# Spreading a feature DFT over the main loop of a DFT-and-attention kernel, one group a round, with sixteen pairs of sequence DFT a round behind it

## The chip, the core and the metric

The kernel runs on one core of a Trainium2 chip. The metric is the device time of one execution in microseconds. The kernel before the change took 1862.16 us, the median of 3 runs (1861.99 to 1862.94). The work is done by five engines with a queue each: PE (matrix products), DVE (vector work), ACT (activations), POOL (general elementwise work) and SP, which issues all transfers here. Each engine takes its queue strictly in order.

## The reference

```
# x: S=2048 tokens, D=640 features; 32 heads of width 20, one shared k and v
a = einsum("bsd,ed->bse", x, dft_hid_re)          # feature DFT
b = einsum("bsd,ed->bse", x, dft_hid_im)
A = einsum("ts,bse->bte", dft_seq_re, a) - einsum("ts,bse->bte", dft_seq_im, b)
q, k, v = x @ wq, x @ wk, x @ wv                  # q in 32 heads
p = softmax(q k^T / sqrt(20))
B = (p v, heads joined) @ wo
g = sigmoid((x * gate_w).sum(-1))
return g * A + (1 - g) * B
```

## The kernel before, in words

Precision comes from splitting each factor into a high and a low part in a 32-bit format that PE multiplies fast; a product is three matmuls (high by high, high by low, low by high). Half-height matmuls with 64 rows of weights run in pairs, one in the upper and one in the lower row group of PE; in the code, `y0` and `y1` are the two halves of one such pair. The order on PE, ACT, DVE and POOL is the order of the program; that of the transfers on SP (all issued by `move`, L106) is chosen by the framework's scheduler.

The stages are these. First come the projections q, k, v and the gate (L114 to L116). Then comes the feature DFT (`ab`, L125): 16 token tiles, 4 groups each of 15 pairs of 64x320 matmuls; between them run the first score maxima. The main loop has 256 rounds: 16 pairs of heads, two halves of the queries (qh) and 8 steps over the keys (kk). A round holds:

- `b` (`b_unit`, L647): eight score products of 512 columns; ACT takes the exponential (L655) into `pt`.
- `a` (`a_unit`, L319): eight score products for the next pair of heads, of which DVE takes the row maxima (L326). The exponentials need those maxima first, since they are subtracted inside `b` as two more rows of `qs`.
- `y` (L551): 12 pairs of the sequence DFT, 64x320 each, with coefficients `ch` and `cl` that POOL splits (L397, L398) from `craw`. A y block is 128 tokens of output with four series of eight tiles; 96 pairs, in two passes (`sh`) over halves of the input tokens. `E` copies out a finished block (ACT L556), and POOL adds (L561, in the second pass also L565).
- `V` (`av_step`, L659): the products of `pt` with v, full height, two per round, which stand apart.

`ROUND` (L737) is the list of these steps, written by hand; `ROUND_LAST` serves the last pair of heads, which has no `a`, and splits each V in half-height steps `W` (L676). Scores go to five banks named S0 to S4, `y` to F0 and F1, V to one bank.

The maxima of a pair of heads are ready when its last `a` is reduced. `a_reduce` and then `a_final` (L336) run some ticks later, a tick being a fixed step of the round: a transpose on DVE (`mt`), a cast and a subtraction on POOL (`ms`, L341 and L342), a write to DRAM (`m_d`) and four reads back into rows 60, 61, 124 and 125 of `qs` (L349). `LEAD` = 12 says by how many units of `a` the maxima run ahead of the loop; four units are a round. `load_c` loads and splits a coefficient tile. It uses three slots in turn, and is called after the first and after the third series of a block for the next block. The slot of the second call is that of a tile which the block's fourth series still reads.

After the loop the output stage multiplies by wo (L114 to L116).

Of the kernel before, what the change touches and what calls it, by code (L numbers as in the profile page):

```python
# [33 lines left out]
def kernel(  # L34
# [46 lines left out]
    m_d = dram.tile([NPAIR, P, 2, 32], F32, name="m_d")  # L81
# [48 lines left out]

    cw = ExitStack()
    w2 = cw.enter_context(tc.tile_pool(name="w2", bufs=1, side="right"))
    x2 = cw.enter_context(tc.tile_pool(name="x2", bufs=2, side="right"))
    wh, wl = [], []

    def load_w(i):
        w_v = (wrT, wiT)[i].rearrange("(c p) n -> p c n", p=P)
        h = w2.tile([P, KC, D], F32R, name=f"wh{i}")
        l = w2.tile([P, KC, D], F32R, name=f"wl{i}")
        for c in range(KC):  # L140
            raw = w2.tile([P, D], F32, name="wraw", bufs=2)
            move(raw, w_v[:, c])
            split(raw, h[:, c], l[:, c])
        wh.append(h)
        wl.append(l)


    T2 = list(range(SJ, NT)) + list(range(SJ))
    xraw, xspl = {}, {}

    def load_x2(it):
        if it < NT:
            t = T2[it]
            xraw[it] = x2.tile([P, KC, P], F32, name="xr2")
            move(xraw[it], xT_v[:, :, t * P : (t + 1) * P])

    def split_x2(it):
        if it < NT:
            h = x2.tile([P, KC, P], F32R, name="xh2")
            l = x2.tile([P, KC, P], F32R, name="xl2")  # L160
            split(xraw.pop(it), h, l)
            xspl[it] = (h, l)


    with ExitStack() as c1:
# [78 lines left out]
        for c in range(KC):  # L244
            if c:
                load_x1(0, c)
            raw = w2.tile([P, D], F32, name="wraw", bufs=2)
# [15 lines left out]
        for n in range(1, 4):  # L263
# [7 lines left out]
            if n == 3:  # L271
                load_x2(0)
                load_x2(1)
                split_x2(0)
# [6 lines left out]
            if n < 3:  # L281
                load_w(n - 1)
# [10 lines left out]
    qsp = ctx.enter_context(tc.tile_pool(name="qsp", bufs=1))  # L293
    sml = ctx.enter_context(tc.tile_pool(name="sml", bufs=2))

    qs = {}
    qbuf = [qsp.tile([P, S], F32R, name=f"qs{i}") for i in range(3)]

    def load_qs(p):
        t = qbuf[p % 3]  # L300
        qs[p] = t
        for hh in range(2):
            r = slice((2 * p + hh) * DH, (2 * p + hh + 1) * DH)
            b = 64 * hh
            move(t[b : b + 20], qh_d[r])
            move(t[b + 20 : b + 40], qh_d[r])
            move(t[b + 40 : b + 60], ql_d[r])

    mx = {}

    def a_unit(u, hh, tag="A"):

        p, r = divmod(u, 64)
        qb, c = divmod(r, 4)
        if r == 0 and p not in mx:
            mx[p] = sml.tile([P, 2, NT, 4], F32, name="mx")
# [4 lines left out]
            qs[p][b : b + 60, qb * P : (qb + 1) * P],  # L321
# [4 lines left out]
        nc.vector.tensor_reduce(mx[p][:, hh, qb, c : c + 1], ps, axis=AX.X, op=ALU.max)  # L326

    mxr = {}

    def a_reduce(p):  # L330
        mxr[p] = sml.tile([P, 2 * NT], F32, name="mxr")
        nc.vector.tensor_reduce(
            mxr[p], mx.pop(p).rearrange("p h q c -> p (h q) c"), axis=AX.X, op=ALU.max
        )

    def a_final(p):  # L336
# [3 lines left out]
        nc.vector.transpose(mt, mxr.pop(p))  # L340
        nc.gpsimd.tensor_copy(ms[:, 0], mt)  # L341
        nc.gpsimd.tensor_tensor(ms[:, 1], mt, ms[:, 0].bitcast(F32), op=ALU.subtract)  # L342
        move(m_d[p], ms)

        m_v = m_d[p].rearrange("(g h b) i t -> h i b g t", g=4, h=2)
        for hh in range(2):
            for i in range(2):
                r = 64 * hh + 60 + i
                move(qs[p][r : r + 1].rearrange("o (b g t) -> o b g t", g=4, t=32), m_v[hh, i : i + 1])  # L349
# [18 lines left out]
    def a_half(hh, tag="A"):  # L368
# [7 lines left out]
        if u % 64 == 16 and u // 64 + 1 < NPAIR:  # L376
            load_qs(u // 64 + 1)
# [12 lines left out]
    def load_c(sh, tb, i):  # L390
# [8 lines left out]
        return h, l  # L399

    first_c = {}


    ab = {}
    later_ab = []
# [472 lines left out]
```

## Time and profile before

| | us |
|---|---|
| median of 3 runs | 1862.16 |
| span of the profiled execution | 1860.4 |
| PE busy | 1846.3 |
| DVE busy | 1449.3 |
| ACT busy | 1269.3 |
| POOL busy | 391.9 |
| reduces of the maxima (L326, 2048) | 1316.3 |

The profiled execution shows one run, 1.8 us under the median. PE's row counts the time in which any matmul runs; two half-height matmuls that overlap count once. A row of the time line gives start, length, engine, line of the source, operation, output from inputs, shapes and, in brackets, the idle time ahead of it with what ended it. In the table by stage a row is a window, its length, the busy time (with counts) of PE, its weight loads, DVE, ACT and POOL, the granted clock, and the transfers' share and rate.

### The profile page before, as it was taken

The page shows a single profiled execution, that of the slowest core. Times are in us where ns is not written, and L with a number is a line of the kernel's source. Part 1 is how long each engine was busy: PE and PEld are TensorE (multiplying, and loading weights), DVE is VectorE, ACT ScalarE, POOL GpSimd, SP SyncE. Part 2 cuts the span into 40 slices and gives each one's busy share as a digit, 9 for nine tenths or more (in the row PEclk, how much of TensorE's full clock was granted, in tenths as well). Part 3 has the DMA queues.
Part 4 walks back from the last instruction along what each step waited for, and adds up shares of the span by engine and source line. Part 5 has one row for each costly group of instructions (what it writes and reads, how often), then busy time and mean ns, then how long its engine had stood idle before and what let it go on. Part 6 is the DMA issues. An engine that isn't in the chain of part 4 may idle for free.

```text
span 1860.4 us, 42326 instructions
## 1 busy us (share of the span) xinstructions
PE 1846.3 (99%) x17368; PEld 1228.9 (66%) x17368; DVE 1449.3 (78%) x2307; ACT 1269.3 (68%) x2425; POOL 391.9 (21%) x336
## 2 busy tenths in 40 slices
PE   8999999999999999999999999999999999999999
PEld 6799986566566656656655665665566566566689
DVE  4469988888888888888888888888888888883144
ACT  4333357777777777777777777777777777778830
POOL 0033431111111111111111222222222212221132
PEclk9999999999999999999999999999999999999999
DMA  7684111211112021212114412121212121111366
GB/s 246 180 262 169 42 37 41 58 42 49 51 33 67 26 61 30 57 33 63 37 56 156 172 50 64 49 65 49 64 49 61 46 65 49 44 49 39 94 203 231
DMA packets 89023, 150.64 MB, mean 81 GB/s; under 512 B 21620, under 2 KB 58484, under 8 KB 86308
## 3 DMA queue, kind: packets, MB, share of 16 engines
q1 hardware_dynamic: 88828, 147.93, 25.8%
q8 instruction: 136, 2.23, 0.5%
q14 instruction: 59, 0.48, 0.1%
HBM read 103.91 MB, written 48.23 MB: 82 GB/s over the span
## 4 chain that ended last, share of the span: by engine, by line
PE 96%; DMA 2%; SPq 1%; DVE 1%; ACT 0%; issue 0%; POOL 0%; ACTq 0%; DVEq 0%
PE av L659 26%; PE y L551 23%; PE b L647 16%; PE a L319 16%; PE ab L125 7%; PE av L676 2%; PE o L114 1%; PE o L116 1%; PE o L115 1%; SPq L106 1%; PE q L116 1%; PE q L114 1%; PE q L115 0%; DMA ql_d<-ql 0%; DMA wraw<-in_wiT_dram 0%; DMA wraw<-in_wrT_dram 0%
## 5 line engine op out<-in xcount | busy, mean ns | idle before, releaser
L326 DVE TENSOR_REDUCE mx<-a 128x1 f32<-128x512 f32 x2048 | 1316.3, 686 | 217.1 <-PE a L319 124.3
L655 ACT ACTIVATE pt<-b 128x512 f32<-128x512 f32 x2048 | 1099.7, 599 | 358.6 <-PE b L647 352.5
L319 PE MATMUL a<-ks,qs 60*128 60x512 f32 x2048 | 755.8, 430 | 0.2 <-ACT pt L655 0.2
L551 PE MATMUL y<-ab,ch 64*128 64x320 f32 x4096 | 688.2, 307 | 1.2 <-DVE both L441 1.2
L647 PE MATMUL b<-qs,ks 62*128 62x512 f32 x2048 | 685.2, 407 | 0.7 <-ACT pt L655 0.7
L551 PEld LDWEIGHTS y<-ab,ch 64*128 64x128 f32 x4096 | 569.5, 186 | 12.8 <-DVE both L441 1.5
L659 PE MATMUL av<-pt,vsb 128*32 128x512 f32 x3840 | 511.3, 605 | 0.0
L647 PEld LDWEIGHTS b<-qs,ks 62*128 62x128 f32 x2048 | 331.8, 187 | 219.0 <-ACT pt L655 218.2
L319 PEld LDWEIGHTS a<-ks,qs 60*128 60x128 f32 x2048 | 335.0, 184 | 198.9 <-ACT pt L655 198.2
L551 PE MATMUL y<-ab,cl 64*128 64x320 f32 x2048 | 456.0, 308 | 0.0
L551 PEld LDWEIGHTS y<-ab,cl 64*128 64x128 f32 x2048 | 347.1, 187 | 0.8
L659 PEld LDWEIGHTS av<-pt,vsb 128*32 128x32 f32 x3840 | 76.0, 108 | 154.8 <-issue 146.5
L561 POOL TENSOR_TENSOR yt<-yt,yu 128x320 f32<-128x320 f32 x64 | 56.8, 888 | 575.6 <-ACT yt L556 563.2
L397 POOL CAST ch<-craw 128x1024 fp32r<-128x1024 f32 x62 | 64.4, 1039 | 477.1 <-PE a L319 441.3
L398 POOL TENSOR_TENSOR cl<-craw,ch 128x1024 fp32r<-128x1024 f32 x62 | 147.7, 2383 | 5.0
L125 PE MATMUL ab<-wh,xh 64*128 64x320 f32 x640 | 134.6, 308 | 1.5 <-DVE gz L235 1.1
L125 PE MATMUL ab<-wl,xh 64*128 64x320 f32 x640 | 134.1, 306 | 0.0
L125 PE MATMUL ab<-wh,xl 64*128 64x320 f32 x640 | 133.8, 306 | 0.0
L410 POOL TENSOR_TENSOR ab<-both,ab 128x320 fp32r<-128x320 f32 x64 | 60.3, 948 | 189.5 <-DMA craw<-in_cre_dram 99.9
L125 PEld LDWEIGHTS ab<-wh,xl 64*128 64x128 f32 x640 | 96.4, 185 | 0.0
L125 PEld LDWEIGHTS ab<-wl,xh 64*128 64x128 f32 x640 | 96.2, 185 | 0.0
L440 ACT ACTIVATE half<-ab 128x320 f32<-128x320 f32 x64 | 28.0, 437 | 88.4 <-PE ab L125 88.4
(86 smaller groups left out, 967.3 us busy)
## 6 DMA issues: line engine op xcount, KB each, us to landing
craw<-in_cre_dram SPq DMA_DIRECT2D x32, 512.0 KB
craw<-in_cim_dram SPq DMA_DIRECT2D x32, 512.0 KB
qs<-qh_d SPq DMA_DIRECT2D x64, 160.0 KB
ab_d<-ab SPq DMA_DIRECT2D x16, 640.0 KB
y_d<-yt SPq DMA_DIRECT2D x64, 160.0 KB
ab<-ab_d SPq DMA_DIRECT2D x16, 640.0 KB
xr<-in_xT_dram SPq DMA_DIRECT2D x20, 256.0 KB
xr<-in_xT_dram SPq DMA_DIRECT2D x16, 320.0 KB
```

Of the source, the lines that this page charges most:

```text
L114: nc.tensor.matmul(ps, wh, xh, start=(i == 0), stop=False)
L125: nc.tensor.matmul(ps, w[r], x[r], start=(i == 0 and k == 0), stop=(i == n - 1 and k == 2))
L319: nc.tensor.matmul(ps, qs[p][b : b + 60, qb * P : (qb + 1) * P], ks[b : b + 60, c * ROW : (c + 1) * ROW], start=True, stop=True,)
L326: nc.vector.tensor_reduce(mx[p][:, hh, qb, c : c + 1], ps, axis=AX.X, op=ALU.max)
L397: eng.tensor_copy(h, raw)
L398: eng.tensor_tensor(l, raw, h.bitcast(F32), op=ALU.subtract)
L410: nc.gpsimd.tensor_tensor(lo, both, hi.bitcast(F32), op=ALU.subtract)
L551: nc.tensor.matmul(ps, w, x, start=start, stop=stop)
L561: nc.gpsimd.tensor_tensor(yt, yt, yu, op=ALU.add)
L647: nc.tensor.matmul(ps, ks[b : b + 62, kc * P : (kc + 1) * P], qs[p][b : b + 62, qc * ROW : (qc + 1) * ROW], start=True, stop=True,)
L655: nc.scalar.activation(t, ps, AF.Exp, scale=SCALE)
L659: nc.tensor.matmul(ps[32 * g : 32 * g + 32, :], vsb[:, kc, :], t, start=first, stop=last)
```

## The change

The feature DFT is now a stream of 64 groups of 15 pairs, ordered in four phases by half of the tokens and half of the columns (`ab_stream`). Sixteen groups run ahead of the loop with 80 `a`; the other 48 run in the first 48 rounds, one in each. After them come 144 rounds with 16 pairs of `y` (three rounds for half a block, six for a block), then 12 pairs a round: 54 rounds with `a`, 10 without. There are four lists: AB15, Y16, Y12 and N12. In each the two V stand side by side at the end. The last pair of heads uses V too, and W is gone. Weights and tokens of the feature DFT are loaded and split per phase, the splits on POOL. Sums of a group (`ab_sum`) are made on POOL after two ACT copies.

The maxima now run by half pairs, v = 2 x pair + query half, 32 of them, 8 rounds each. `qs` has four buffers of half the length. `LEAD` is 8 units, `a_reduce` comes one tick and `a_final` two ticks after the last `a`, and a tick is now every second `b`.

The core of the diff:

```diff
-    m_d = dram.tile([NPAIR, P, 2, 32], F32, name="m_d")
+    m_d = dram.tile([2 * NPAIR, P, 2, 32], F32, name="m_d")
...
-        if u % 64 == 16 and u // 64 + 1 < NPAIR:
-            load_qs(u // 64 + 1)
-        if u % 64 == 63:
-            later(1, a_reduce, u // 64)
-            later(3, a_final, u // 64)
+        v, r = divmod(u, UV)
+        if r == 8 and v + 1 < 2 * NPAIR:
+            load_qs(v + 1)
+        if r == UV - 1:
+            later(1, a_reduce, v)
+            later(2, a_final, v)
...
+    def ab_sum(grp):
+        t0, t1 = grp["t"]
+        half, e, t, i, hi, lo = grp["ab"]
+        nc.gpsimd.tensor_tensor(t0, t0, t1, op=ALU.add)
+        if stage["loop"]:
+            nc.gpsimd.tensor_copy(hi, t0)
+        else:
+            nc.scalar.activation(hi, t0, AF.Copy)
+        nc.gpsimd.tensor_tensor(lo, t0, hi.bitcast(F32), op=ALU.subtract)
...
+    Y16 = (
+        "b0S1 a1S0 a0S3 b1S4 y0 y1 y0 y1 y0 y1 y0 y1 y0 b1S2 y0 a1S1 y0 y0 a1S0 y0 b1S4 y0 y0 y1 y0 b1S3 y0 y1 "
+        "a0S2 y1 b0S1 y1 y1 y0 y1 y0 y1 b0S4 y1 a0S0 y1 y1 b0S3 y1 a0S2 y1 a1S1 y0 E0 E1 V V"
+    ).split()
...
+    LEAD = 8
+    NL = 2 * (UV + LEAD)
+    KL = 15 * 2 * SJ
...
+    NAB = 3 * 2 * SJ
+    Y3 = 48
+
+    def plan_of(n):
+        if n < NAB:
+            return AB15
+        if n < NAB + 3 * Y3:
+            return Y16
+        return Y12 if state[1] < NA else N12
```

`load_c` keeps its three slots and its two calls per block.

Three places in the order of instructions follow. On PE before, at the end of a round, with `av` the V products (now L734), `a` (now L368) and `b` (now L722) the scores:

```order
L319 MATMUL a_0_7568<-ks,qs_865 128x512 [waits Activation_49]
L659 MATMUL av_0_7110<-pt,vsb 32x512 x4
L319 MATMUL a_0_7575<-ks,qs_865 128x512 [waits Activation_49]
L319 MATMUL a_1_7583<-ks,qs_865 128x512 [waits DVE_49]
L647 MATMUL b_13_1_0_7586<-qs_867,ks 128x512 [waits Activation_49]
L647 MATMUL b_13_0_1_7590<-qs_867,ks 128x512
L659 MATMUL av_0_7110<-pt,vsb 32x512 x4
L647 MATMUL b_13_1_1_7598<-qs_867,ks 128x512 [waits Activation_49]
```

And in the changed kernel, at the end of round 71, with the last y's of a block ahead of the V's and the first b of half pair v = 9 behind them:

```order
L541 MATMUL y_3_1_1_9371<-ab_5044,ch 128x320
L368 MATMUL a_0_9653<-ks,qs_108 128x512 [waits DVE_49]
L541 MATMUL y_3_1_1_9371<-ab_5044,cl 128x320
L368 MATMUL a_1_9657<-ks,qs_108 128x512 [waits Activation_49]
L541 MATMUL y_3_1_0_9370<-ab_5044,cl 128x320
L734 MATMUL av_0_9045<-pt,vsb 32x512 x8
L722 MATMUL b_0_2_0_9675<-qs_107,ks 128x512 [waits DMAHW1_49,DMAHW0_49,DVE_49]
L368 MATMUL a_1_9679<-ks,qs_108 128x512
L368 MATMUL a_0_9682<-ks,qs_108 128x512 [waits Activation_49]
L722 MATMUL b_0_2_1_9691<-qs_107,ks 128x512 [waits DMAHW3_49,DMAHW2_49]
```

The two av stand together; the b behind them waits for two transfers, the reads of the maxima.

On POOL before, around the maxima of a pair, `ch` and `cl` being the split of a coefficient tile and `yt` the sum of a block's halves:

```order
L397 CAST ch<-craw 128x1024 [waits DMAHW5_49]
L398 TENSOR_TENSOR cl<-craw,ch 128x1024 [waits Pool_49]
L561 TENSOR_TENSOR yt<-yt,yu 128x320 [waits DMAHW6_49,Activation_49]
L341 CAST ms<-mt 128x32 [waits DVE_49]
L342 TENSOR_TENSOR ms<-mt,ms 128x32 [waits Pool_49]
L397 CAST ch<-craw 128x1024 [waits DMAHW3_49,PE_49]
L398 TENSOR_TENSOR cl<-craw,ch 128x1024 [waits PE_49,Pool_49]
```

On POOL now, around the maxima of half pair 9 (round 70):

```order
L551 TENSOR_TENSOR yt<-yt,yu 128x320 [waits DMAHW2_49,Activation_49]
L442 CAST ch<-craw 128x1024 [waits DMAHW2_49,PE_49]
L443 TENSOR_TENSOR cl<-craw,ch 128x1024 [waits PE_49,Pool_49]
L387 CAST ms<-mt 128x32 [waits DMAHW1_49,DVE_49]
L388 TENSOR_TENSOR ms<-mt,ms 128x32 [waits Pool_49]
L551 TENSOR_TENSOR yt<-yt,yu 128x320 [waits DMAHW3_49,Activation_49]
```

The two ms rows have moved from ahead of the ch that waits for PE to behind it and its cl.

On SP before, the four reads of the maxima (1x64x32) stand right behind their write:

```order
L106 DMA m_d<-ms 128x64 [waits DMAHW5_49,Pool_49]
L106 DMA qs_865<-m_d 1x64x32 [waits DMAHW6_49,DMAHW5_49]
L106 DMA qs_865<-m_d 1x64x32 [waits DMAHW7_49]
L106 DMA qs_865<-m_d 1x64x32 [waits DMAHW0_49]
L106 DMA qs_865<-m_d 1x64x32 [waits DMAHW1_49]
```

On SP now, for half pair 25 in the second pass over the tokens, where `y_d<-yt` writes a block's sum and `y_23491` loads the first pass's part of another:

```order
L106 DMA m_d<-ms 128x64 [waits DMAHW0_49,Pool_49]
L106 DMA y_d<-yt 128x320 [waits DMAHW1_49,Pool_49]
L106 DMA y_23491<-y_d 128x320 [waits DMAHW2_49]
L106 DMA craw<-in_cim_dram 128x1024
L106 DMA qs_107<-m_d 1x32x32 [waits DMAHW4_49,DMAHW0_49]
L106 DMA qs_107<-m_d 1x32x32 [waits DMAHW5_49]
L106 DMA qs_107<-m_d 1x32x32 [waits DMAHW6_49]
L106 DMA qs_107<-m_d 1x32x32 [waits DMAHW7_49]
```

Three transfers stand between the write and the reads now; in the first pass it is two, the sum's write (to `y0_d`) and a craw.

More of the change, by code (lines that the diff above doesn't have):

```diff
@@ L148 @@
[L148 to L162, printed above, removed]
+    qsp = ctx.enter_context(tc.tile_pool(name="qsp", bufs=1))
@@ L568 @@
     ended = []
+    stage = {"loop": False}
+    def ab_sum(grp):
[4 more added lines that the diff above has]
+            nc.gpsimd.tensor_copy(hi, t0)
+        else:
+            nc.scalar.activation(hi, t0, AF.Copy)
+        nc.gpsimd.tensor_tensor(lo, t0, hi.bitcast(F32), op=ALU.subtract)
+        if half == 1 and i == 1:
+            j = t - SJ
+            later(3, move, ab_d[j, e], ab[j, e].rearrange("p a b -> p (a b)"))
     def y_evict(g):
@@ L594, in f_stream @@
     def f_stream():
+        yield from ab_stream()
+        cw.close()
+        yp.append(ctx.enter_context(tc.tile_pool(name="yp", bufs=2, side="right")))
         cur = {}
```

390 lines of the change are left out of this document (217 added, 173 removed).

## The prediction

> **What bounds the kernel now.** I read the page's busy shares first.
>
> ```profile
> PE 1846.3 (99%) x17368; PEld 1228.9 (66%) x17368; DVE 1449.3 (78%) x2307; ACT 1269.3 (68%) x2425; POOL 391.9 (21%) x336
> ```
>
> Then the busy time by stage (window; its length; busy time of PE, weight loads, DVE, ACT and POOL; clock; DMA).
>
> ```profile
> 0.00:98.60 98.60, 90.92 (x406) 71.97 (x406) 41.00 (x65) 38.88 (x71) 4.06 (x10) 1.00 0.73 219
> 98.60:257.40 158.80, 157.26 (x2043) 156.73 (x2043) 135.25 (x237) 61.87 (x144) 62.75 (x67) 1.00 0.40 128
> 257.40:1704.20 1446.80, 1445.93 (x13408) 878.76 (x13408) 1224.81 (x1942) 1098.23 (x2071) 289.40 (x241) 1.00 0.19 57
> 1704.20:1783.50 79.30, 79.28 (x1001) 50.53 (x1001) 15.47 (x18) 68.54 (x138) 14.77 (x12) 1.00 0.37 114
> 1783.50:1860.40 76.90, 72.89 (x513) 70.90 (x512) 32.77 (x46) 1.77 (x4) 20.94 (x9) 1.00 0.67 219
> ```
>
> PE waits nowhere in the loop: 1445.93 us busy of 1446.80. The stages are projections, feature DFT with the first maxima, 240 rounds, the last pair's 16 rounds, and output: 98.6 + 158.8 + 1446.8 + 79.3 + 76.9 = 1860.4, the profiled execution. The median of the runs, 1862.16, lies 1.8 above; I add that at the end. While PE is the bound, a round costs what its matmuls cost in order, so I read one round.
>
> ```profile
> 284.31 1.07 PE L659 MATMUL av<-pt,vsb 128*32 128x512 f32 x8
> 285.30 0.50 PE L319 MATMUL a<-ks,qs 60*128 60x512 f32 x2
> 285.64 0.41 PE L647 MATMUL b<-qs,ks 62*128 62x512 f32 x2
> 285.97 1.07 PE L659 MATMUL av<-pt,vsb 128*32 128x512 f32 x8
> 286.97 0.50 PE L647 MATMUL b<-qs,ks 62*128 62x512 f32 x1
> ...
> 290.34 0.64 PE L659 MATMUL av<-pt,vsb 128*32 128x512 f32 x4
> ```
>
> The price of a half-height pair comes from the DFT stage, the first and last of forty rows:
>
> ```profile
> 99.18 0.31 PE L125 MATMUL ab<-wh,xh 64*128 64x320 f32 x2
> ...
> 104.90 0.31 PE L125 MATMUL ab<-wh,xh 64*128 64x320 f32 x2
> ```
>
> And once, where the last pair begins, two V's already stand together:
>
> ```profile
> 1706.32 1.92 PE L659 MATMUL av<-pt,vsb 128*32 128x512 f32 x16
> 1708.17 0.50 PE L647 MATMUL b<-qs,ks 62*128 62x512 f32 x2
> ```
>
> Half-height matmuls run in two row groups at once. Forty rows of L125 from 99.18 to 104.90 give 5.72 / 39 = 0.1467 us for a pair 320 wide; 512 wide is 1.6 times that, 0.2347. A V takes 0.99 (284.31 to 285.30) or 1.00. Between the V's stand two a and two b, 0.469 by that price, but 0.67 pass: 0.20 is lost where half-height work drains into a V. The other piece, 286.97 to 290.34, is 12 y pairs and 6 of 512: 1.760 + 1.408 = 3.17, again 0.20 short of 3.37. Round: 290.34 - 284.31 = 6.03. Two V's side by side occurred once: 1708.17 - 1706.32 = 1.85.
>
> **The sum without new waits.** The two V's together spare one drain and 0.14 more: a round costs (pairs x 0.1467) + (a's and b's per row group x 0.2347) + 0.20 + 1.85. Bounds of the gain are 0.14 (no drain spared) and 0.34. I take 0.34, since both pieces show the drain.
>
> - 48 rounds of 15 feature pairs, 8 per row group: 2.20 + 1.88 + 2.05 = 6.13, together 294.2.
> - 144 rounds of 16 pairs: 6.275, together 903.6.
> - 54 rounds of 12: 5.69, together 307.3.
> - 10 rounds of 12 without a's: 4.75, together 47.5.
>
> That is 1552.6 for all 256 rounds. Ahead of them remain 240 pairs and 80 maxima. PE would need 240 x 0.1467 + 40 x 0.2347 = 44.6, but DVE reduces longer:
>
> ```profile
> 631.46 2.10 ACT L655 ACTIVATE pt<-b 128x512 f32<-128x512 f32 x4 [0.36 <-PE b L647]
> ...
> 631.50 1.95 DVE L326 TENSOR_REDUCE mx<-a 128x1 f32<-128x512 f32 x3 [0.42 <-PE b L647]
> ```
>
> The loop's start, on PE:
>
> ```profile
> 257.41 0.42 PE L551 MATMUL y<-ab,ch 64*128 64x320 f32 x2 [1.19 <-DVE both L441]
> ```
>
> Three in a row take 1.95, 0.65 each, so 80 take 52. In the loop, 8 reduces are 5.2 and 8 exponentials (2.10 for four) 4.2; both fit under 5.69, DVE with little to spare. At the loop's start the kernel waits 1.19 now. Afterwards the sums and splits of feature groups go through POOL, and ACT's copy waits there ahead of the exponentials. Four casts and subtractions of the next weights stand ahead of one sum; from POOL's rows below (1.04 and 2.38 at 1024 wide) I scale them to about 5.4, so 5.5, with bounds 1 and 8. The splits during the rounds hide under PE: POOL is busy 289 of 1446.8. Projections and output stay, 98.6 and 76.9: the two left-over V's equal the four W halves.
>
> Sum: 98.6 + 52 + 5.5 + 1552.6 + 76.9 = 1785.6, 74.8 below the execution. The last W's go at no cost, since the round formula holds V's instead.
>
> **The new wait.** A half pair's maxima leave DVE (mt), pass POOL (ms), go to DRAM (m_d) and come back as rows of qs, which the first b reads. The order shows the cast ch and subtraction cl ahead of ms on POOL whenever the second coefficient load of a y block falls into the round of a_final. That ch overwrites a slot which the block's last y still reads.
>
> ```profile
> 591.86 1.04 POOL L397 CAST ch<-craw 128x1024 fp32r<-128x1024 f32 x1 [21.47 <-PE a L319]
> 592.98 2.38 POOL L398 TENSOR_TENSOR cl<-craw,ch 128x1024 fp32r<-128x1024 f32 x1
> 595.31 0.88 POOL L561 TENSOR_TENSOR yt<-yt,yu 128x320 f32<-128x320 f32 x1
> ```
>
> PE's V right behind, and then the maxima's chain on POOL and SP elsewhere:
>
> ```profile
> 592.06 0.64 PE L659 MATMUL av<-pt,vsb 128*32 128x512 f32 x4
> ...
> 629.08 0.21 POOL L341 CAST ms<-mt 128x32 fp32r<-128x32 f32 x1 [10.40 <-DVE mt L340]
> 629.37 0.25 POOL L342 TENSOR_TENSOR ms<-mt,ms 128x32 fp32r<-128x32 f32 x1
> 629.65 0.34 SPq L106 DMA_DIRECT2D m_d<-ms  x1
> 631.15 2.51 SPq L106 DMA_DIRECT2D qs<-m_d  x4
> ```
>
> The landing of another small read, and what single issues cost SP:
>
> ```profile
> 1753.01 1.17 SPq L106 DMA_DIRECT2D sm<-sum_d  x2
> 1755.92 0.25 DVE L727 RECIPROCAL rc<-sm 128x16 f32<-128x16 f32 x1 [12.94 <-DMA sm<-sum_d]
> 1138.10 0.90 SPq L106 DMA_DIRECT2D craw<-in_cre_dram  x2
> 1176.89 0.42 SPq L106 DMA_DIRECT2D y<-y_d  x1
> ```
>
> ch waited 21.47 us for PE (the named a is only the last event before it; the block's last y's go out just ahead of V). Before, ms stood in front of that ch, with a whole pair's period aligned to two blocks, so the wait hurt nobody. Now the maxima are ready two rounds before b, but ms lies behind ch until the block ends, and where that round is the fifth of six (16-pair rounds) or the seventh of eight (12-pair rounds), the block ends exactly where b must start. Half pair v has a_final in round 8v - 2. Blocks of six start at round 48: v = 9, 12, 15, 18, 21, 24 coincide. Blocks of eight start at 192: all of v = 25 to 30. That is 12 stalls; the last one splits on DVE and is free.
>
> One stall, from T, where ch starts (591.86, 0.2 before V at 592.06): b's natural place is T + 0.16 + 1.85 = 2.0. ch and cl end near 3.5, ms at 4.0. SP issues m_d; the first read follows 631.15 - 629.65 = 1.5 later. Before it stand, on SP, y0_d behind yt (0.88) and a craw (0.45): reads start at 5.8. Two reads are 2 x 0.63, their landing 1.2 (m_d's own: 1.50 - 0.34), so b starts at 8.25, and the other row group's b makes 0.65 more: 6.9 late. In the second y half the sum has one more POOL step (0.88) and y0's load (0.42): 7.7. Three of 6.9, one of 7.5 and one of 8.2 (the reload of ab and a longer queue), seven of 7.7: 90.3. Bounds: 5.5 each (one read, no queue ahead) and 9.5 (landing as for sm: 1755.92 - 1753.01 - 1.17 = 1.74 on both trips, one more sum), 66 and 114.
>
> Behind the late b stand a's and y's on PE, ACT's exponentials and DVE's reduces; nothing else feeds PE, so each stall is an idle PE. What a matmul costs after such an idle, the start shows:
>
> ```profile
> 5.85 0.79 PE L114 MATMUL kv<-xh,kvgh 128*128 128x512 f32 x1 [5.85 <-ACT kvgh L109]
> ...
> 9.43 0.58 PE L116 MATMUL q<-xh,wql 128*128 128x512 f32 x1
> 9.84 0.39 PE L114 MATMUL q<-xh,wqh 128*128 128x512 f32 x1
> 10.07 0.40 PE L115 MATMUL q<-xl,wqh 128*128 128x512 f32 x1
> ```
>
> After 5.85 us of idle, nine matmuls take 9.84 - 5.85 = 3.99, 0.44 each; then one takes 0.23. That lost 3.99 - 9 x 0.233 = 1.9 us. Whether the idle or the program's start made it, the trace can't tell: bounds 0 and 1.9 per stall. My idles are 6.2 us and more, so I take 1.9: 12 x 1.9 = 22.8. The granted clock reads 1.00 in the first window all the same, so that row doesn't show this slowness.
>
> The Trainium skill, in "TensorE: Matmul & The Clock Gate", section "Part 1: The HAM clock gate", says that an idle window of about 3.4 us halves PE's clock, and about 3.4 us of activity restores it. By that each stall would lose an estimated 1.7, 20 in all in place of 22.8; it agrees with the row at the start and speaks for the upper bound.
>
> Sum: 1785.6 + 90.3 + 22.8 = 1898.7, and 1.8 for the median: **1900**. Bounds of the unknown terms around it: stalls -24 / +24, slow restart -23, loop start -4 / +3.
>
> **The rivals.**
> - *No slow restart.* The start's slowness belongs to the start alone: 1785.6 + 90.3 + 1.8 = 1878. For it: nothing later in the trace shows slow matmuls, though no idle there comes near 6 us. Chance 0.17.
> - *The chain is short, the gain stays.* The place is SP's queue between ms and b. The stalls decide: the gain of 74.8 is gone at 6.2 us each, all told. At the lower bound of 5.5 and no slow restart the time is 1785.6 + 66 + 1.8 = 1853, faster; if the reads overlap other work still more, down to 1787 with none. For it: the two trips have been measured only apart. Against: ch and cl alone take 3.5. Chance 0.15, 0.11 of it faster, 0.04 within 0.2%.
> - *Rounds get longer.* DVE has 5.2 of 5.69 us, five banks serve 16 scores between two pairs of V. A wait of 0.12 per round gives 31 more: 1931. Against: PE idles 0.87 in the whole present loop (1446.80 - 1445.93), with banks as few. Chance 0.12.
> - *The change doesn't do what it says.* The V pair spares no drain (0.14 per round): 0.20 x 246 = 49 more, 1949. Against: the row at 1706.32. Chance 0.05.
>
> **How the numbers follow.** The forecast, 1875 to 1925 by its bounds, has 0.51. Something like 0.2% (3.7 us) is what a measurement of this kernel can tell from no change; slower sums to 0.51 + 0.17 + 0.12 + 0.05 = 0.85, same 0.04, faster 0.11. The range 1857 to 1932 leaves out the short chain and the lost drain, some 0.18.
>
> **What would show it.** PE's waits for qs rows at b about 12 times, 6 to 8 us each, every third half pair at first and each of the last six; on POOL ms starting right after a cl that waited for PE; rounds between stalls of 6.13, 6.28, 5.69 and 4.75; the loop's first b near 98.6 + 52. After a stall matmul pairs near 0.28 in place of 0.147 for some 4 us, or not. I am wrong if b doesn't wait (then near 1787), if stalls last under 5 us, or if PE waits in ordinary rounds.

## The result and the profile after

The changed kernel took 1943.76 us, the median of 4 runs (1941.94 to 1945.78), beside 1862.45 for the kernel before on the same chip: a ratio of 1.0438 (95% interval 1.0423 to 1.0452). The forecast was 1900, in a range of 1857 to 1932, and the result lies above it: the sign was right, the size about half. The profiled execution spans 1944.0, 45.3 more than the 1898.7 that the steps added up to.

The page of the changed kernel, with each engine's busy time and the granted clock in 40 slices:

```profile
PE 1817.1 (93%) x17112; PEld 1318.4 (68%) x17112; DVE 1377.8 (71%) x2249; ACT 1236.5 (64%) x2420; POOL 568.3 (29%) x561
...
PEclk9998999999999999999899899999989999888999
```

PE is busy for 29 us less than before, with 256 matmuls fewer, and yet the span is 84 us longer: PE now waits. The dips in the clock mark where. The stages, in the columns of the table before (projections; feature DFT with the first maxima; its 48 rounds; the 144 rounds with 16 pairs; 12 pairs; the last pair of heads; output):

```profile
0.00:102.70 102.70, 92.72 (x388) 72.51 (x390) 40.66 (x53) 32.47 (x60) 22.04 (x24) 0.97 0.67 212
102.70:159.18 56.48, 47.57 (x553) 45.78 (x550) 49.70 (x88) 23.94 (x55) 38.39 (x41) 1.00 0.44 145
159.18:466.60 307.42, 303.05 (x3012) 216.68 (x3016) 245.90 (x405) 242.81 (x494) 187.19 (x223) 0.98 0.24 75
466.60:1431.70 965.10, 919.04 (x9212) 656.87 (x9208) 731.25 (x1198) 648.58 (x1266) 228.75 (x199) 0.97 0.21 68
1431.70:1792.50 360.80, 308.17 (x2746) 209.61 (x2746) 243.92 (x409) 226.32 (x424) 59.84 (x58) 0.92 0.13 41
1792.50:1872.00 79.50, 78.02 (x753) 48.69 (x751) 36.77 (x58) 61.74 (x123) 16.09 (x13) 1.00 0.37 118
1872.00:1944.00 72.00, 68.55 (x469) 68.21 (x465) 29.60 (x44) 0.60 (x1) 16.04 (x6) 1.00 0.64 206
```

Some 46 us of PE's idle time lie in the fourth stage and 53 in the fifth, where before it idled 0.87 in the whole loop. The last row starts at the end of the left-over V pair; from the first product of the output, at 1867.83, it takes 76.2, near the 76.9 forecast. What PE waits for, from the list of waits (engine and line, releaser, total, count, longest):

```profile
PE b L722 <- DMA qs<-m_d: 101.2, 15, 10.5
```

Twelve of these 15 waits are the stalls that the prediction counted, v = 9, 12, 15, 18, 21, 24 and 25 to 30, of 6.55 to 10.49 us, 98.3 together; two of the others belong to the loop's start, and one of 0.39 lies in round 176. The first, from the time line (SPq rows are SP's own queue; a group's length is that of its issues):

```profile
610.46 1.04 POOL L442 CAST ch<-craw 128x1024 fp32r<-128x1024 f32 x1 [16.40 <-PE y L541]
611.58 2.35 POOL L443 TENSOR_TENSOR cl<-craw,ch 128x1024 fp32r<-128x1024 f32 x1
613.88 0.21 POOL L387 CAST ms<-mt 128x32 fp32r<-128x32 f32 x1
614.16 0.25 POOL L388 TENSOR_TENSOR ms<-mt,ms 128x32 fp32r<-128x32 f32 x1
614.44 0.35 SPq L106 DMA_DIRECT2D m_d<-ms  x1
615.25 0.34 SPq L106 DMA_DIRECT2D y_d<-yt  x1
615.64 0.42 SPq L106 DMA_DIRECT2D craw<-in_cre_dram  x1
616.17 2.77 SPq L106 DMA_DIRECT2D qs<-m_d  x4
619.14 0.76 PE L722 MATMUL b<-qs,ks 62*128 62x512 f32 x1 [6.55 <-DMA qs<-m_d]
```

ch waited 16.40 us for the block's last y; ms follows right behind cl; the write, two other transfers and the four reads follow on SP; then b goes out. And the clock around this stall (window, length, the five busy times, clock, transfers):

```profile
612.00:614.00 2.00, 0.59 (x8) 0.00 (x0) 0.05 (x1) 0.00 (x0) 2.00 (x2) 1.00 0.05 20
616.00:618.00 2.00, 0.00 (x0) 0.00 (x0) 0.00 (x0) 0.00 (x0) 1.92 (x2) 0.94 0.86 293
618.00:620.00 2.00, 0.86 (x3) 0.50 (x3) 0.02 (x1) 0.00 (x0) 0.63 (x1) 0.50 0.19 59
620.00:622.00 2.00, 1.99 (x13) 1.69 (x14) 1.26 (x2) 1.19 (x2) 0.00 (x0) 0.50 0.90 305
622.00:624.00 2.00, 2.00 (x16) 2.00 (x15) 0.94 (x2) 0.69 (x2) 0.00 (x0) 0.50 0.13 47
624.00:626.00 2.00, 2.00 (x23) 2.00 (x22) 1.30 (x3) 1.84 (x4) 0.00 (x0) 0.85 0.00 0
```

PE idles from 612.6, the clock halves a little before 618 and comes back after 624. At 0.50 PE starts 13 and 16 matmuls in 2 us, against 23 later. All told, a round with a stall lasts 9.47 to 12.54 longer than an ordinary one; the twelve sum to 124.6, that is 98.3 of idle and 26.3 behind it.

Ordinary rounds, measured from V pair to V pair, take 6.15 (15 pairs; forecast 6.13), 6.27 (16; 6.275), 4.745 (12 without a's; 4.75), but 6.05 with 12 pairs and a's, where 5.69 was forecast. One such round, on PE, DVE and ACT:

```profile
1437.74 1.92 PE L734 MATMUL av<-pt,vsb 128*32 128x512 f32 x16
...
1440.16 4.89 DVE L375 TENSOR_REDUCE mx<-a 128x1 f32<-128x512 f32 x8 [1.18 <-PE a L368]
1440.19 4.33 ACT L730 ACTIVATE pt<-b 128x512 f32<-128x512 f32 x8 [1.74 <-PE a L368]
...
1443.79 0.64 PE L734 MATMUL av<-pt,vsb 128*32 128x512 f32 x4
```

PE shows no wait here: its loss is spread in small pieces. DVE makes its eight reduces without a gap, starts 0.57 after the V pair's end (1437.74 + 1.85) and has idled 1.18 ahead of them; 4.89 and some 1.17 are the 6.05. ACT does likewise, 4.33 and 1.74.

Last, the stretch ahead of the loop: a wait in the projections, DVE's first reduces, two waits at the loop's first b's, and the exponentials behind ACT's copy of a group, which waits for POOL's sum.

```profile
57.36 0.50 PE L114 MATMUL kv<-xh,kvgh 128*128 128x512 f32 x1 [2.15 <-ACT xh L109]
...
106.66 15.04 DVE L375 TENSOR_REDUCE mx<-a 128x1 f32<-128x512 f32 x25 [2.38 <-DMA qs<-qh_d]
...
159.18 0.47 PE L722 MATMUL b<-qs,ks 62*128 62x512 f32 x1 [1.69 <-DMA qs<-m_d]
160.57 0.76 PE L722 MATMUL b<-qs,ks 62*128 62x512 f32 x1 [0.88 <-DMA qs<-m_d]
...
163.95 0.47 ACT L569 ACTIVATE ab<-abt 128x320 fp32r<-128x320 f32 x1 [5.75 <-POOL abt L565]
...
164.96 0.79 PE L368 MATMUL a<-ks,qs 60*128 60x512 f32 x1 [2.16 <-ACT pt L730]
```

The first feature group starts at 101.71; the steps let the projections end at 98.6, which makes 3.1. From there to the loop's first b, at 159.18, it takes 57.5 where the steps have 52, 5.5 more: the 80 reduces take 52, but the first starts only at 106.66. The first V pair of the loop starts at 176.12. The steps give 98.6 + 52 + 5.5, and 8.6 for the first round, which has no V pair yet, and the second up to its own; so it comes 11.4 late.

So the 45.3 us are 54 x 0.36 = 19.4 for the 12-pair rounds, 124.6 - 113.1 = 11.5 for the stalls, 11.4 ahead of the loop, and 3 in small pieces. In these 3 a slip of the sum is taken off: it has a V pair in each of the 256 rounds and one more in the output, 257 where the kernel has 256, so 1.85 too much.

### The profile page after: what moved, and what is told of

Read it like the earlier page. It is cut to its first block, busy times and chain, and to the rows that moved or that the text cites. A ratio compares the mean times of both kernels' runs of the same rounds, so it can differ in the third digit from the quotient of the medians.

```text
span 1944.0 us, 42803 instructions
## 1 busy us (share of the span) xinstructions
PE 1817.1 (93%) x17112; PEld 1318.4 (68%) x17112; DVE 1377.8 (71%) x2249; ACT 1236.5 (64%) x2420; POOL 568.3 (29%) x561
## 4 chain that ended last, share of the span: by engine, by line
PE 88%; POOL 4%; DMA 4%; SPq 2%; issue 1%; DVE 1%; ACT 0%; POOLq 0%; DVEq 0%
PE av L734 23%; PE y L541 21%; PE b L722 18%; PE a L368 14%; PE ab L541 7%; DMA qs<-m_d 2%; SPq L106 2%; POOL cl L443 2%; PE o L114 1%; PE o L115 1%; PE o L116 1%; PE q L114 1%; PE q L116 1%; PE q L115 1%; DMA wraw<-in_wq_dram 1%
## 5 line engine op out<-in xcount | busy, mean ns | idle before, releaser
L722 PE MATMUL b<-qs,ks 62*128 62x512 f32 x2048 | 790.4, 423 | 104.1 <-DMA qs<-m_d 101.2
L368 PE MATMUL a<-ks,qs 60*128 60x512 f32 x2048 | 742.0, 419 | 5.2 <-DVE mx L375 3.0
L541 PE MATMUL y<-ab,ch 64*128 64x320 f32 x4096 | 735.9, 312 | 0.0
L722 PEld LDWEIGHTS b<-qs,ks 62*128 62x128 f32 x2048 | 361.3, 190 | 331.1 <-DVE mx L375 173.6
L541 PE MATMUL y<-ab,cl 64*128 64x320 f32 x2048 | 519.7, 311 | 0.0
L734 PE MATMUL av<-pt,vsb 128*32 128x512 f32 x4096 | 492.5, 598 | 0.0
L368 PEld LDWEIGHTS a<-ks,qs 60*128 60x128 f32 x2048 | 360.8, 189 | 12.3 <-ACT pt L730 3.3
L734 PEld LDWEIGHTS av<-pt,vsb 128*32 128x32 f32 x4096 | 106.8, 109 | 223.6 <-issue 215.1
L565 POOL TENSOR_TENSOR abt<-abt,abu 128x320 f32<-128x320 f32 x64 | 55.8, 872 | 185.3 <-ACT abu L587 185.3
L541 PE MATMUL ab<-wbh,xh 64*128 64x320 f32 x256 | 60.4, 309 | 0.0
L541 PE MATMUL ab<-wbh,xl 64*128 64x320 f32 x256 | 60.1, 308 | 0.0
L570 POOL TENSOR_TENSOR ab<-abt,ab 128x320 fp32r<-128x320 f32 x64 | 56.1, 877 | 13.1 <-ACT ab L569 7.0
L541 PE MATMUL ab<-w0h,xl 64*128 64x320 f32 x192 | 49.6, 316 | 4.2 <-POOL xl L218 4.2
L541 PE MATMUL ab<-w0l,xh 64*128 64x320 f32 x192 | 51.4, 311 | 0.0
L541 PE MATMUL ab<-w1l,xh 64*128 64x320 f32 x192 | 50.9, 306 | 0.0
```

The costliest lines, as they stand in the source:

```text
L368: nc.tensor.matmul(ps, qs[v][b : b + 60, qb * P : (qb + 1) * P], ks[b : b + 60, c * ROW : (c + 1) * ROW], start=True, stop=True,)
L541: nc.tensor.matmul(ps, w, x, start=start, stop=stop)
L565: nc.gpsimd.tensor_tensor(t0, t0, t1, op=ALU.add)
L570: nc.gpsimd.tensor_tensor(lo, t0, hi.bitcast(F32), op=ALU.subtract)
L722: nc.tensor.matmul(ps, ks[b : b + 62, kc * P : (kc + 1) * P], qs[2 * p + qc // 2][b : b + 62, (qc % 2) * ROW : (qc % 2 + 1) * ROW], start= ...
L734: nc.tensor.matmul(ps[32 * g : 32 * g + 32, :], vsb[:, kc, :], t, start=first, stop=last)
```

## The experiments

**The stalls: maxima split on DVE.** The theory says that they come from ms standing behind ch on POOL, so ms goes to DVE.

```diff
-        nc.gpsimd.tensor_copy(ms[:, 0], mt)
-        nc.gpsimd.tensor_tensor(ms[:, 1], mt, ms[:, 0].bitcast(F32), op=ALU.subtract)
+        nc.vector.tensor_copy(ms[:, 0], mt)
+        nc.vector.tensor_tensor(ms[:, 1], mt, ms[:, 0].bitcast(F32), op=ALU.subtract)
```

> The changed kernel with one edit: the cast and the subtraction that make ms of a half pair's maxima run on DVE, right behind the transpose, so they no longer stand behind the ch and cl that wait for PE. Theory (ms behind ch on POOL is what delays the first b of 12 half pairs; each costs 8.2 us of idle and about 2.2 of slow clock behind it, 124.6 us in all by the length of the 12 rounds): the 12 waits vanish, 1944 - 125 = 1819 us, with the clock at 1.00 in the loop. Rival (the chain of DRAM write and reads on SP, not POOL, is too long for two rounds of lead): the waits stay at 6 us or more, over 1930 us.

1843.79 us, ratio 0.9900 (0.9886 to 0.9915) to the kernel before; the twelve long waits are gone. Of the 25 us missing to the expectation most are given back in the rounds of `a_final`. One of them, in DVE's rows and PE's V pairs:

```profile
1419.83 1.92 PE L734 MATMUL av<-pt,vsb 128*32 128x512 f32 x16
...
1423.46 0.20 DVE L386 STREAM_TRANSPOSE mt<-mxr 128x32 f32<-128x32 f32 x1
1423.69 0.18 DVE L387 CAST ms<-mt 128x32 fp32r<-128x32 f32 x1
1423.91 0.19 DVE L388 TENSOR_TENSOR ms<-mt,ms 128x32 fp32r<-128x32 f32 x1
...
1426.42 1.07 PE L734 MATMUL av<-pt,vsb 128*32 128x512 f32 x8
```

That round takes 6.59 in place of 6.05; over the half pairs it is 0.45 to 1.35 each, some 19 together. Two rounds whose first b still waits 0.6 to 0.7 for the reads (v = 19 and 22) give 2.3 more, and the loop's first V pair starts at 177.95, 1.8 later than in the changed kernel. Half a microsecond of DVE between reduces lengthens the round by as much: a first sign that DVE has no slack there.

**The stalls: a longer lead.** `ms` stays on POOL and behind ch, but a round earlier.

```diff
-    LEAD = 8
+    LEAD = 12
```

> The changed kernel with one number changed: maxima run ahead by 12 units (three rounds) in place of 8 (two). Theory (a third round of slack takes the chain off the path, and in the 12-pair part the maxima then come ahead of the second coefficient load): no waits of b over 1 us in the loop; 16 more reduces ahead of the loop cost 16 x 0.65 = 10, two rounds of 6.05 turn into two of 4.75, so 1944 - 125 + 10 - 3 = 1826 us. Rival (the order on POOL doesn't matter, the chain as such is too long by a fixed time): waits fall by one round of 6 us only, to 2 or 3 us each, about 1860 us.

1823.47, ratio 0.9793 (0.9778 to 0.9807), and no b waits for qs in the rounds. Taking away the stalls, and with them the idle and the slow restart, is worth 120 us, near the 124.6 to which the longer rounds sum up; the loop's first V pair comes 1.8 later, behind the 16 maxima more.

**The slow restart.** Matmuls without use fill the gaps, so that PE is busy through each stall.

```diff
+    FILL = {8 * v: 26 if v < 18 else 32 for v in (9, 12, 15, 18, 21, 24, 25, 26, 27, 28, 29, 30)}
...
+        fill = FILL.get(ROUNDS.index(rnd) + 1, 0)
+        if fill:
+            spin = psum.tile([P, ROW], F32, tag="F0", name="spin", bufs=1)
+            for i in range(fill):
+                nc.tensor.matmul(spin, ks[:, :P], ks[:, :ROW], start=True, stop=True)
```

> The changed kernel with 26 or 32 extra matmuls of 128x512 (0.23 us each at full clock, 6.1 or 7.5 us) into an idle bank at the end of each of the 12 rounds ahead of a late b; their result is read by nothing. Theory (after an idle of 6 us and more the clock falls to half and stays there for over 5 us, which costs 2.2 us a time; the extra matmuls fit into the idle and keep the clock up): granted clock 1.00 behind these rounds, 12 x 2.2 = 26 less, 1918 us. Rival (the slow restart is the refill of DVE and ACT and not the clock): no gain, 1944 us or above.

1931.03, 12.7 less than the changed kernel; the ratio to before is 1.0368 (1.0348 to 1.0389). Two of the windows of above, in this kernel:

```profile
618.00:620.00 2.00, 1.03 (x5) 0.32 (x4) 0.39 (x1) 0.38 (x1) 0.30 (x1) 1.00 0.27 61
620.00:622.00 2.00, 1.99 (x23) 2.00 (x25) 1.31 (x3) 1.42 (x3) 0.00 (x0) 1.00 0.82 301
```

The clock stays at 1.00, and 23 matmuls start where 13 did. From the late b to the next V pair, summed over the twelve, 76.9 has become 57.6: 19.4 of the 26.3 were the clock, although in two stalls 2.1 and 3.3 us stayed unfilled and the clock still fell. The waits themselves grew by 2.8, so the total fell by less than expected. That the idle makes the slow restart is shown.

**The V pair by itself.** The kernel before with the list Y12 of the changed one, so only the rounds' order is new.

```diff
-        "y0 y1 y0 a1S0 b0S2 y1 b1S3 y0 y0 y1 y0 y1 y0 a1S1 y0 b0S4 y1 y1 y0 y1 y0 y1 y0 y1 "
-        "a0S2 y1 y1 b0S3 a1S0 y0 y0 y1 b1S1 E1 a0S4 V a0S3 a1S0 E0 b0S1 b1S2 V b1S1 a0S4"
+        "b0S0 a1S3 a0S4 y1 y1 b0S1 y1 y0 b1S2 y1 y0 y0 a1S0 b0S3 y1 y0 y1 y0 a1S1 y0 y0 b1S4 y0 y1 y0 a1S2 "
+        "b0S0 y0 y1 y1 a0S3 y1 b1S4 a0S1 y0 y1 y1 y0 b1S2 a0S0 E0 E1 V V"
```

> The kernel before with one edit: its round's list is the 12-pair list of the change, with the two V side by side; everything else stays (feature DFT ahead of the loop, whole pairs of maxima, lead of 12). Theory (with the V's together no score can be made for 1.85 us, so 16 scores have to pass five banks in the rest of the round; DVE and ACT set that, and a round of 12 pairs can't fall under 6.05 us): no gain, 240 x (6.05 - 6.03) = +5, 1867 us. Rival (the prediction's formula, a round costs its matmuls and one drain): 240 x 0.34 less, 1781 us.

1872.51, ratio 1.0056 (1.0039 to 1.0073).

```profile
503.95 1.92 PE L659 MATMUL av<-pt,vsb 128*32 128x512 f32 x16
...
510.03 1.92 PE L659 MATMUL av<-pt,vsb 128*32 128x512 f32 x16
```

6.08 from pair to pair, where V's apart gave 6.03. At 12 pairs the gain of 0.34 doesn't appear. (The list also places y and the banks differently, so this alone doesn't say that the V pair is the reason.) The next runs ask why. Each changes `lead_12`, so that no stall interferes, and all but `v_apart` only in its 12-pair rounds.

**Is it DVE?** Reduces over 256 of 512 columns.

```diff
-        nc.vector.tensor_reduce(mx[v][:, hh, qb, c : c + 1], ps, axis=AX.X, op=ALU.max)
+        wide = HALF_ROW[0]
+        nc.vector.tensor_reduce(mx[v][:, hh, qb, c : c + 1], ps[:, :wide], axis=AX.X, op=ALU.max)
```

> The kernel of lead_12 with one edit: in the rounds of the 12-pair list with a's, DVE reduces only the first 256 of the 512 columns of each score tile (the maxima of the later half of each tile are left out). Theory (a 12-pair round takes 6.05 and not 5.69 because DVE's eight reduces of 0.61 hold the banks that the next scores need; ACT's eight exponentials at 0.54 hold them less): with reduces of about 0.35 the 12-pair rounds fall to 5.7, 52 x 0.35 = 18 less, 1805 us. Rival (something else in that list, such as the two drains at its V's or ACT alone, sets 6.05): the rounds stay at 6.05, 1823 us.

1821.53, ratio 0.9781 (0.9762 to 0.9801): no change, rounds of 6.02. DVE has gaps now, but ACT doesn't:

```profile
1491.71 4.33 ACT L732 ACTIVATE pt<-b 128x512 f32<-128x512 f32 x8 [0.85 <-PE a L369]
1497.73 2.56 ACT L732 ACTIVATE pt<-b 128x512 f32<-128x512 f32 x5 [1.69 <-PE a L369]
```

Eight exponentials without a gap, 1.69 idle, 6.02 in all.

**Is it the order of the banks?** `half_reduce` with two banks exchanged.

```diff
-        "b0S0 y0 y1 y1 a0S3 y1 b1S4 a0S1 y0 y1 y1 y0 b1S2 a0S0 E0 E1 V V"
+        "b0S0 y0 y1 y1 a0S3 y1 b1S2 a0S1 y0 y1 y1 y0 b1S4 a0S0 E0 E1 V V"
```

> The kernel of half_reduce (12-pair rounds reduce only the first 256 of the 512 columns of a score tile) with one edit more: in the 12-pair list the last two b of row group 1 swap their banks, S4 and S2. In half_reduce the rounds stayed at 6.02: ACT's eight exponentials ran back to back from 0.57 after the V's, and the seventh b stood for S4, which the fifth b's exponential frees. Theory (a bank that a score holds until ACT or DVE has read it is what sets the 12-pair round, after 1.85 us of V's in which no score can be made): with the swap the seventh b takes a bank that a short reduce has freed, and the rounds fall to about 5.75, 52 x 0.27 = 14 less, 1807 us. Rival (the floor lies elsewhere, not in banks): still 6.02, 1821 us.

1831.02, ratio 0.9833 (0.9813 to 0.9852), rounds of 6.22: longer by 0.20, where shorter was expected. The order of the banks moves the round, so they matter; which one binds was guessed wrongly.

**Is there room for more y?** Two pairs run a second time ahead of the seventh b.

```diff
-        "b0S0 y0 y1 y1 a0S3 y1 b1S4 a0S1 y0 y1 y1 y0 b1S2 a0S0 E0 E1 V V"
+        "b0S0 y0 y1 y1 a0S3 y1 d0 d1 d0 d1 b1S4 a0S1 y0 y1 y1 y0 b1S2 a0S0 E0 E1 V V"
```

> The kernel of lead_12 with one edit: in the 12-pair list with a's, two pairs of y are run a second time (added once more into their sums, so y is counted twice there), right ahead of the seventh b; 14 pairs a round. half_swap moved the round to 6.22, so the swap of a bank does matter, but not as I had said, and what sets the floor of 6.05 is still argued only. Theory (the scores' banks, in turn with ACT and DVE, set a floor of about 6.05, below which PE's own work, 5.98 with 14 pairs, hides): the rounds stay at 6.05 to 6.1, 1823 to 1826 us. Rival (a round costs its matmuls and 0.36 of something fixed): 6.34 a round, 52 x 0.29 = 15 more, 1838 us.

1832.68, ratio 0.9841 (0.9824 to 0.9857), rounds of 6.25. Of 0.29 more work 0.20 shows: the time lost in a round isn't free where these were put. Both sides missed.

**ACT, and ACT with DVE.** The exponentials over half the columns (`half_exp`), and the reduces as well (`half_both`, with the edit of `half_reduce` too).

```diff
-        nc.scalar.activation(t, ps, AF.Exp, scale=SCALE)
-        pt[(hh, kc, qc)] = t
+        part = HALF_EXP[0]
+        nc.scalar.activation(t[:, :part], ps[:, :part], AF.Exp, scale=SCALE)
+        pt[(hh, kc, qc)] = t if part == ROW else t[:, :part]
...
+        wide = t.shape[-1]
+        for c in range(0, ROW, wide):
+            nc.tensor.matmul(ps[rows, c : c + wide], vsb[:, kc, :], t, start=first and not c, stop=last and c + wide == ROW)
```

> lead_12 with the exponentials of the 12-pair rounds made over 256 of the 512 columns; the V of such a round is made in two pieces of 256 columns that both read those 256 (the other half of each score is left out). Every product on PE, and every reduce on DVE, keeps its size. Theory: a 12-pair round is held up by its five score banks. Between two pairs of V 16 scores must pass through five banks; ACT frees one each 0.53 us and DVE one each 0.61, starting 0.57 after the V's, and at least eleven must be free again before the last score can be written: 0.57 + 11 / (1/0.53 + 1/0.61) = 3.69, then the last score, the drain and the V pair: some 6.0 in all, where 6.05 was measured. With ACT's part at some 0.33 the eleven take 2.36, and what limits then is DVE's share of the banks in the fixed order and the row groups of PE: about 5.85 a round, 53 x 0.20 = 11 us less than lead_12, some 1813. Rival: the loss is PE's own, in the drain around the V pair; then the rounds stay at 6.05 and the time at 1823. If the V in pieces is longer than 1.85 for a pair, that is read from its rows and taken off.

> The same, and the reduces of these rounds over 256 of 512 columns too (half of the exponentials and of the maxima left out). Theory of the banks: with both consumers shorter no bank is waited for and PE's own order is left: 12 pairs and 8 scores per row group, in the order of the list, in which two y of one row group stand together at places; walked through in order with 0.1467 and 0.2347 a row group that is 3.78 in place of 3.64, so 5.75 to 5.85 a round and 53 x 0.20 to 0.30 = 11 to 16 us less than lead_12: 1807 to 1813. With reduces alone halved the round had stayed at 6.02. Rival (PE's drain): 6.05 and 1823.

`half_exp` took 1820.23, ratio 0.9768 (0.9752 to 0.9785), `half_both` 1803.70, ratio 0.9680 (0.9665 to 0.9694). In `half_exp` the round stays at 6.03, where 5.85 was expected (5.98 if the 0.05 that its V pair in pieces takes longer, see below, is taken off); it is DVE now that has no gap:

```profile
1509.59 4.88 DVE L375 TENSOR_REDUCE mx<-a 128x1 f32<-128x512 f32 x8 [0.96 <-PE a L368]
1515.62 4.88 DVE L375 TENSOR_REDUCE mx<-a 128x1 f32<-128x512 f32 x8 [1.16 <-PE a L368]
```

In `half_both` both have gaps, and the round falls to 5.73 (V pairs, then DVE's first reduces of a round):

```profile
1503.13 1.97 PE L741 MATMUL av<-pt,vsb 128*32 128x256 f32 x32
1508.86 1.97 PE L741 MATMUL av<-pt,vsb 128*32 128x256 f32 x32
...
1511.33 0.76 DVE L377 TENSOR_REDUCE mx<-a 128x1 f32<-128x256 f32 x2 [1.90 <-PE a L369]
```

In pieces the V pair takes 1.90 (its next b starts at 1510.76) in place of 1.85, so without that the round is 5.68: the forecast's 5.69 was right for PE alone. The rival, a loss on PE in the drain around V, falls. Either consumer alone holds the round at about 6.0; only with both shortened does it become PE's own. The sum of eleven freed banks, by which `half_exp` should have gained 0.20, isn't how it works: the mean of both consumers doesn't count. That the fixed order lets the slower one count fits the two runs, but no run changed the number of banks.

**Where the V pair pays.** One V of the 16-pair list moves to its middle.

```diff
-... b1S3 y0 y1 a0S2 y1 b0S1 ... y1 a1S1 y0 E0 E1 V V
+... b1S3 y0 V y1 a0S2 y1 b0S1 ... y1 a1S1 y0 E0 E1 V
```

> The kernel of lead_12 with one edit: in the 16-pair list the first of the two V moves from the end to the middle, where both row groups have done the same work. Theory (there PE is the bound, and a second V apart costs one more drain of 0.20 and 0.14 at the V's): 6.27 + 0.34 = 6.61 a round, 144 x 0.34 = 49 more, 1872 us. Rival (the drains are hidden by the banks in any case, the V pair is worth nothing): 1823 us.

1932.56, ratio 1.0377 (1.0357 to 1.0398): rounds of about 7.05, 0.78 longer, where a drain was to cost 0.34. The banks weren't fitted anew, and b waits 55.4 us for reduces, so this tells only that V's apart are not cheaper with these banks. What the pair is worth at 16 pairs stays open.

**Ahead of the loop.** First the copy of a group's sum goes from ACT to POOL throughout (here too on `lead_12`).

```diff
-        if stage["loop"]:
-            nc.gpsimd.tensor_copy(hi, t0)
-        else:
-            nc.scalar.activation(hi, t0, AF.Copy)
+        nc.gpsimd.tensor_copy(hi, t0)
```

> The kernel of lead_12 with one edit: the high part of a feature group's sum is always made on POOL, never on ACT. Theory (at the loop's start ACT stands at such a copy, waits for POOL, which splits weights first, and holds the first exponentials; PE then waits 3 us and runs on at half clock): the wait of a for ACT goes, with its slow clock 4 to 6 us less, 1818 us. Rival (POOL, now with 16 x 0.45 us more ahead of the loop, is itself the late one): no gain or a few us more, 1823 to 1830 us.

1819.19, ratio 0.9770 (0.9754 to 0.9786), 4.3 less than `lead_12`, as expected; the wait of a for ACT, 3.07 there, is gone. Then the loads of the feature DFT's weights, which SP issues early in the projections, are called later.

```diff
-            if n < 3:
-                load_w(n - 1, 0)
-                split_w(n - 1)
+            if n == 2:
+                for i in range(2):
+                    load_w(i, 0)
+                    split_w(i)
```

> The kernel of lead_12 with one edit: both loads and splits of the first phase's feature weights come behind the third token block of the projections, in place of one behind the second and one behind the third. Theory (the early load goes ahead of the writes of q and k on SP's queue, which delays them by 7 us, and so ACT, the next tokens' split and PE by 2 to 3 us with slow clock behind it; the projections end 4 us later than before the change): projections end near 98.6 again, 1819 us. Rival (it is the 1.9 us of PE waiting alone): 1821.5 us; or the loads are late for the feature DFT in turn: 1825 us or more.

1822.25, ratio 0.9785 (0.9771 to 0.9800): nothing, since the scheduler puts them on SP as early as before; it doesn't test the cause. So they and the first two token loads leave SP's queue for ACT's (on `pool_copy`):

```diff
+    queue = {"of": nc.sync}
...
-        nc.sync.dma_start(words(dst), words(src))
+        queue["of"].dma_start(words(dst), words(src))
...
+                queue["of"] = nc.scalar
...
+                queue["of"] = nc.sync
```

> The kernel of pool_copy with one edit: the first phase's weight loads and its first two token loads are issued by ACT at their place in the program, not by SP. In late_w the scheduler put them in front of SP's writes of k and q again, so that test said nothing. Theory (those loads, which wait for POOL's splits, hold SP's queue for 7 us and with it the writes that free q's buffers, ACT, and PE at 57 us, with slow clock behind it): the writes of k start near 29 us as in the kernel before, PE's wait of 2.0 + 0.8 at 57 us goes, the projections end 4 us earlier, 1815 us. Rival (the delay comes from the transfers themselves, not from the queue): 1819 us; or ACT, which now waits for POOL's splits at those loads, is late itself: 1821 us or more.

1812.68, ratio 0.9736 (0.9720 to 0.9753), 6.5 less than `pool_copy`. The write of the first keys to `ks` went out ten microseconds earlier, at 26.66 in place of 36.63:

```profile
26.66 0.90 SPq L108 DMA_DIRECT2D ks<-kh  x1
```

The wait at 57 us is gone, and the feature DFT starts at 92.83 in place of 100.22 (94.86 in the kernel before). Not all of these 7.4 us arrive: PE now waits soon behind its start, for reduces that wait for the first rows of qs, and the granted clock is at 0.50 from about 97.3 to 104.1. The loop's first V pair starts 5.4 earlier (169.27 in place of 174.69).

```profile
99.66 3.10 DVE L381 TENSOR_REDUCE mx<-a 128x1 f32<-128x512 f32 x5 [4.26 <-DMA qs<-qh_d]
...
100.41 0.79 PE L374 MATMUL a<-ks,qs 60*128 60x512 f32 x1 [5.07 <-DVE mx L381]
```

Last, this kernel with `LEAD` = 10:

> The kernel of act_loads with one number changed: the lead is 10 units, two and a half rounds, in place of 12. Theory (what matters is on which side of the waiting ch and cl the maxima stand in POOL's queue; with 10 units a_final falls late into the round before the one in which that load is made, so ms stands ahead of it or behind one that is through a round earlier): no waits of b over 1 us in the loop after its start; 8 reduces fewer ahead of the loop, 8 x 0.65 = 5 less, one round with a's more, 1.3 more, 1809 us. Rival (slack as such is what lead 12 gave, and half a round of it is missing now): waits of 1 to 3 us at the 12 half pairs, 1825 to 1850 us.

1811.77, ratio 0.9723 (0.9707 to 0.9740). No b waits for qs, so one more half round of lead would have been enough; but the gain over `act_loads` is 0.9, less than expected and within the scatter of either. It is the best version found, 2.8% faster than the kernel before, and it keeps the spread feature DFT, the V pairs and the half pairs.

## Why the prediction was half right

- **The sum of the rounds.** For 15 and 16 pairs, and for 12 without a's, it held to 0.02. It failed at "both fit under 5.69, DVE with little to spare" and at the 0.34 taken for every round, these among them: 54 x 0.36 = 19.4 us, the largest part of the error. PE's own time was right (5.68 in `half_both`). What the step left out is that a consumer's time isn't the sum of its work alone. During the V pair no score is written; ACT and DVE live on what stands in the five banks and then wait for the first new score, 1.16 to 1.18 on DVE, 1.7 on ACT. So a round is 4.89 + 1.17 for DVE and 4.33 + 1.7 for ACT, both 6.05, and each alone holds it there (`half_reduce`, `half_exp`). Standing side by side the V's save PE a drain and cost the consumers one long pause. In the rows of before, with the V's apart, the pause ahead of three reduces was 0.42. How long the pause must be stays open: it depends on the order of the banks (6.02 in `half_reduce`, 6.22 in `half_swap`), and 6.05 isn't a plain floor, since two more pairs of y bring 6.25 (`fourteen`). Another order of the twelve pairs that fits the V pair better wasn't tried.
- **The rival "Rounds get longer"** named this mechanism, DVE and five banks, and gave it 0.12 a round, in all rounds. It was 0.36, in the 54 with 12 pairs and a's, and 0.02 or less in the others: with 15 and 16 pairs PE alone needs more than 6.05, and the last ten have no reduces.
- **The new wait.** Place, count and order of the twelve stalls were right, and so was the mechanism, as `ms_on_dve` and `lead_12` show from two sides. The size was 90.3 and measured 98.3. The first three came at 6.55 to 6.93 against 6.9, the last six at 7.7 to 10.5 against 7.7. What was too small there is the landing of the reads: the sum gives 2 x 0.63 + 1.2 = 2.46 from the first read's issue to b, and 2.9 to 4.2 pass (1481.00 to 1484.65 for v = 25). In the longest, POOL's next cl also held up a craw that stands ahead of the reads on SP by 2.5 (1718.33), which no step counted. The 6.9 and 7.7 have 0.65 in them for the second row group's b, which here lies in the time behind the stall; both together, 113.1 was forecast and 124.6 came.
- **The slow restart.** 1.9 a stall was taken from the program's start. Behind the stalls 26.3 / 12 = 2.2 are lost, of which `spin_in_stalls` shows at least 19.4 / 12 = 1.6 to be the clock. The rival without it (1878) falls.
- **Ahead of the loop.** "Projections and output stay, 98.6 and 76.9" failed for the projections: loads for the feature DFT stand ahead of the first `ks` writes on SP's queue, and PE waited at 57 us (without them there, `act_loads`, it doesn't): 3.1. By the start of the first feature group it is even 6.9, 101.71 in place of 94.86, since the 98.6 already held that group of the kernel before. The step "80 take 52" held for the reduces, but left out that the first waits for rows of qs and starts 5.0 after the first group: 5.5 up to the loop's first b. And 5.5 for the loop's start left out the b's own wait for their first rows: 2.8. Together 11.4.
- **The other rivals.** The chain wasn't short. That the V pair spares no drain is refuted on PE by `half_both`, though at 12 pairs the kernel gains nothing from it.

## What to carry to other kernels

Where products without results for the consumers are gathered into one block, the consumers' pause there has to be added to their work before one says that they fit: a consumer's round is its work plus the pause that the buffers can't bridge. Small work behind a wait on an in-order engine inherits that wait. Where it feeds the bound engine, give it more lead or another engine: here that was worth 120 and 100 us, more than the 75 that the whole change was to bring. A load added to a queue early in the program can be paid for far later, so look at what stands behind it on that queue.

## What the runs showed of the hardware

- In the first stall the granted clock halved some 5.2 us after PE fell idle (612.6 to about 617.8, from the mean of 0.94 in that window), and came back some 5.5 us after work began again (619.14 to about 624.6). The times aren't fixed: over the twelve stalls it halved 2.1 to 5.3 us after PE fell idle, in six of them before 2.9, and came back 3.4 to 6.4 us after work began. In the third, PE idles from 932.92, and the mean of 0.80 in the window below puts the halving at 935.2, 2.3 later. Each stretch at half clock lasted 6.8, 10.2 or 13.7 us, which is two, three or four times 3.41. The Trainium skill, "TensorE: Matmul & The Clock Gate", section "Part 1: The HAM clock gate", gives about 3.4 us for both; the effect agrees, but half of the idles here halved the clock sooner, and the return took that or longer.

```profile
934.00:936.00 2.00, 0.00 (x0) 0.00 (x0) 0.00 (x0) 0.00 (x0) 1.92 (x5) 0.80 0.07 16
```

- Short idles do it as well: around the wait of 2.15 us at 57 us, with 0.76 more just behind it, the clock is at 0.50 from 58 to 64 us. In `act_loads`, without that wait, it is at 1.00. Not each does: a wait of 3.03 us up to 107.41, in the feature DFT of the changed kernel, left the clock at 1.00.
- Keeping PE busy with useless products while it waited took 19 us off twelve restarts, but the waits grew by 2.8.
